# Attention and two mixtures of experts on one core: raw tiles, sums and differences of the 512-token round, its output units in pairs, and TensorE's order as the code emits it

## The chip, the core and the metric

The kernel runs on one core of a Trainium2 chip. The metric is the device time of one execution in microseconds. Five engines work side by side and in order, each through its own queue of instructions: PE (TensorE, matmuls), ACT (ScalarE), DVE (VectorE), POOL (GpSimd) and SP (SyncE, which here only issues DMAs). They wait for each other by semaphores. TensorE runs at 2.4 GHz when the throttle grants it its full clock, which is shown as 1.00.

## The reference, cut to what matters

Packed attention gives 2304 tokens of 512 numbers, a first layer with a squared relu follows, and then a mixture of eight experts, of which this change touches one part:

```
x = attention(q, k, v, p); x = (relu(x @ w_in) ** 2) @ w_out
logits = x @ w_gate;  P = exp(logits - logits.max())
for _ in range(8):
    P /= P.sum(1) + 1e-09;  P /= P.sum(0) + 1e-09;  P *= N / E
for e in range(E):                       # 8 experts
    h = relu(x @ w1[e])                  # 512 -> 1024
    out += P[:, e:e+1] * (h @ w2[e])     # 1024 -> 512
```

## The kernel before

Numbers are kept to fp32 accuracy by splitting each operand in two fp32r parts, a high part (a copy on ACT) and a low part (a subtraction on POOL or DVE). A product is then three matmuls: high by high, high by low, low by high.

The mixture of experts runs in three rounds of tokens: 512, 768 and 1024. Each round goes through 32 units n = 0 to 31, four to an expert. The change lies in the first round ("the 512-token round", p = 0), which on the timeline runs from about 418 to 776 us. It is also the round in which the weights w1 and w2 come in raw, are summed, split and put away (kept) for the other rounds, and in which the gate P is balanced.

A unit multiplies by Strassen's scheme in Winograd's form: seven block products instead of eight, from sums of weight blocks (S1 to S4, made by `w1_sums`) and differences of token blocks (T1 to T4, made in `operand`, line L466). Each product is six matmuls of 256 columns (L754) into the PSUM tiles X, Y or Z, in the order A11, A12, S1, S2, S4, S3, A22. Between them ACT copies partial results away (s: L815 after A11, L823 after S1, L826 after S2), DVE adds them back (L817 after A12, L830 after S4, L833 after S3), and `evac` makes the relu on ACT (L761) and its low part on DVE (L762), both in the tile hh. Those four hh tiles are the operands of the second layer's output units: `y_unit` makes six matmuls of 512 columns (L784) into one of four PSUM tiles of its own, and every fourth unit adds the sum, times the gate, to acc (L794 on DVE, L790 on ACT for the first expert). `ys` is the list of output units still to be done; `y()` takes one from it. It starts with five empty ones, so that a unit's outputs come one unit or so later.

After A12, S2, S3 and A22 the unit calls hook(n, 0) to hook(n, 3). The hooks issue what stands beside the products: the splits of weights for coming units (`split_w`: ACT L176, POOL L177), loads of raw weights (L111; from ACT's queue, apart from the first two), `sums_ahead` (four sums on DVE, L145 to L148, into one tile "wt"), the putting away of what is split (SP, L181), the operands for the next round (`keep_operand` in units 9 to 15: difference L466, copy L445, low part L446), and the gate. The gate takes the maximum of P in unit 1 (L696 on DVE, matmul L700, L701), spreads it in unit 2, and then balances in eight turns of two steps: `rows_step` on DVE (L714 to L719) and `cols_step` (matmul L724 by a matrix of ones, then L726 to L728 on DVE). Its matmuls take a PSUM tile of the same four ("c") that X, Y and Z turn through.

A scheduler orders each engine's instructions, by its own estimate of when they can run, except where the code says that an instruction comes after another: `pinned()` puts what it holds behind the last instruction so far of every engine. Products and output units are not held by it, so that the scheduler mixes them on PE. EARLY is 10: up to unit 9 sums and loads are placed by the hook itself.

## Time and profile before

| | before |
|---|---|
| median of 3 runs | 1858.34 us (1858.09 to 1859.39) |
| the profiled execution: time (its span, with nothing around it) | 1858.9 us |
| granted clock of TensorE, mean | 0.999 |
| busy share of the span: PE, weight loads, DVE, ACT, POOL | 99%, 89%, 69%, 45%, 56% |

The profile is of one execution, and its times count from the first instruction. A busy time of PE is made from records whose ends are modelled and that overlap with the next matmul, so the start of one group against the start of the next says more about its pace. An idle time is listed before the instruction that waited, with the instruction that released it.

### The profile page before, as it was taken

The numbers are of one execution on the slowest core, as the hardware profiler recorded it, in microseconds if no ns is written. First come the engines' busy times: TensorE is split into PE (matmuls) and PEld (weight loads), VectorE is DVE, ScalarE is ACT, GpSimd is POOL, SyncE is SP. The second block draws the span as 40 slices with busy tenths as digits, with TensorE's granted clock in tenths as the row PEclk, the third lists the DMA queues.
The fourth block names the chain that finished last, engine by engine and source line by source line (L and its number), as shares of the span: only waits on it lengthen the run. The fifth ranks groups of instructions, "written<-read, shape, count | busy, mean of one in ns | idle before, by whom it ended". The sixth has DMA issues, their size and how long they took to land.

```text
span 1858.9 us, 28526 instructions
## 1 busy us (share of the span) xinstructions
PE 1837.6 (99%) x10190; PEld 1663.2 (89%) x10190; DVE 1279.4 (69%) x2097; ACT 829.4 (45%) x1538; POOL 1047.0 (56%) x653
## 2 busy tenths in 40 slices
PE   8999999999999999999999999999999999999999
PEld 7899999998888898888888888888889999999998
DVE  4777777766766555588778877888775666666665
ACT  6667654644555555343333433333334323332323
POOL 3313322435688777278778777778764444444444
PEclk9999999999999999999999999999999999999999
DMA  7402211206789887767777787776788777788874
GB/s 277 159 27 77 69 46 47 103 2 229 252 317 325 299 271 255 243 219 257 234 249 233 233 267 233 238 238 228 248 307 268 276 258 266 258 245 265 267 251 148
DMA packets 166124, 403.55 MB, mean 217 GB/s; under 512 B 14192, under 2 KB 79712, under 8 KB 165984
## 3 DMA queue, kind: packets, MB, share of 16 engines
q1 hardware_dynamic: 131520, 346.15, 55.1%
q10 hardware_dynamic: 34464, 55.58, 9.8%
q8 instruction: 81, 1.33, 0.3%
q14 instruction: 59, 0.48, 0.1%
HBM read 273.96 MB, written 127.72 MB: 216 GB/s over the span
## 4 chain that ended last, share of the span: by engine, by line
PE 91%; DVE 3%; DMA 2%; issue 1%; ACT 1%; POOL 1%; SPq 0%; ACTq 0%; POOLq 0%; DVEq 0%
PE psc L754 35%; PE psx L1141 16%; PE psz L1141 12%; PE psy L430 11%; PE psy L784 7%; PE psh L411 6%; PE psh L364 1%; PE pp L270 1%; DMA raw<-win 1%; POOL w L177 1%; DMA raw<-w 1%; PE s L304 0%; PE s L238 0%; ACT w L176 0%; DMA kt<-kT 0%
## 5 line engine op out<-in xcount | busy, mean ns | idle before, releaser
L754 PE MATMUL psc<-xc,w 128*128 128x256 f32 (+2 forms) x4032 | 777.4, 335 | 2.3 <-ACT s L823 1.6
L754 PEld LDWEIGHTS psc<-xc,w 128*128 128x128 f32 x4032 | 666.3, 188 | 67.5 <-ACT s L823 1.8
L1117 POOL TENSOR_TENSOR hh<-hb,hh 128x1024 fp32r<-128x1024 f32 (+1 forms) x224 | 504.6, 2257 | 372.1 <-ACT hh L1116 314.4
L1116 ACT ACTIVATE hh<-hb 128x1024 fp32r<-128x1024 f32 (+1 forms) x224 | 213.8, 955 | 447.8 <-DVE hb L1114 197.8
L1141 PE MATMUL psx<-hh,wa 128*128 128x512 f32 (+1 forms) x1536 | 352.7, 362 | 0.0
L1141 PEld LDWEIGHTS psx<-hh,wa 128*128 128x128 f32 x1536 | 278.9, 188 | 30.2 <-ACT hh L1116 0.4
L1141 PE MATMUL psz<-hh,wa 128*128 128x512 f32 (+1 forms) x1152 | 261.9, 362 | 0.3 <-issue 0.3
L1141 PEld LDWEIGHTS psz<-hh,wa 128*128 128x128 f32 x1152 | 209.0, 188 | 23.2 <-issue 0.9
L430 PE MATMUL psy<-h,w 128*128 128x320 f32 (+2 forms) x1200 | 224.8, 331 | 0.2
L784 PE MATMUL psy<-w,hh 128*128 128x512 f32 x768 | 201.5, 395 | 3.9 <-ACT hh L761 3.3
L177 POOL TENSOR_TENSOR w<-raw,w 128x512 fp32r<-128x512 f32 (+1 forms) x128 | 157.9, 1255 | 76.9 <-ACT w L176 66.0
L1149 DVE TENSOR_TENSOR acc<-psx,acc 128x512 f32<-128x512 f32 (+1 forms) x248 | 152.1, 618 | 70.2 <-PE psx L1141 69.0
L430 PEld LDWEIGHTS psy<-h,w 128*128 128x128 f32 x1200 | 189.0, 188 | 12.2 <-ACT x L436 0.7
L1149 DVE TENSOR_TENSOR acc<-psz,acc 128x512 f32<-128x512 f32 (+1 forms) x184 | 112.6, 618 | 93.1 <-PE psz L1141 93.0
L1047 DVE SCALAR_TENSOR_TENSOR hb<-psc,gate 128x512 f32<-128x512 f32 (+1 forms) x256 | 157.3, 620 | 12.2 <-PE psc L754 7.3
L1021 POOL TENSOR_TENSOR wa<-rb,wa 128x512 fp32r<-128x512 f32 x80 | 132.6, 1666 | 49.9 <-ACT wa L1020 39.5
L784 PEld LDWEIGHTS psy<-w,hh 128*128 128x128 f32 x768 | 135.1, 189 | 27.8 <-ACT hh L761 4.6
L1114 DVE TENSOR_TENSOR hb<-hb 128x1024 f32<-128x1024 f32 (+1 forms) x96 | 133.5, 1390 | 28.9 <-POOL hh L1117 28.0
L411 PE MATMUL psh<-at,g 128*128 128x320 f32 (+2 forms) x768 | 123.4, 297 | 0.2 <-DVE r L417 0.2
L411 PEld LDWEIGHTS psh<-at,g 128*128 128x128 f32 x768 | 110.9, 189 | 4.3 <-DVE r L417 0.4
L177 POOL TENSOR_TENSOR w<-wt,w 128x512 fp32r<-128x512 f32 x64 | 83.7, 1316 | 47.8 <-ACT w L176 35.9
L129 POOL TENSOR_TENSOR ca<-ca,cc 128x512 int32<-128x512 int32 x28 | 36.7, 1311 | 102.6 <-ACT cc L128 94.1
(155 smaller groups left out, 1843.3 us busy)
## 6 DMA issues: line engine op xcount, KB each, us to landing
w<-kept_w SPq DMA_DIRECT2D x184, 512.0 KB, 4.8
kept_w<-wa SPq DMA_DIRECT2D x112, 512.0 KB, 4.6
wa<-kept_w SPq DMA_DIRECT2D x112, 512.0 KB, 4.8
kept_w<-w SPq DMA_DIRECT2D x96, 512.0 KB, 4.7
raw<-w ACTq DMA_DIRECT2D x58, 512.0 KB, 5.2
rb<-w ACTq DMA_DIRECT2D x64, 256.0 KB, 4.5
w<-kept_w SPq DMA_DIRECT2D x61, 256.0 KB, 4.3
raw<-win SPq DMA_DIRECT2D x16, 512.0 KB, 3.9
```

What stands on the lines that cost most here:

```text
L177: nc.gpsimd.tensor_tensor(w[:, 1, :n], t, w[:, 0, :n].bitcast(F32), op=ALU.subtract)
L411: nc.tensor.matmul(ps[:, u - begin:w - begin], gw[:, x, m * 128:(m + 1) * 128], at[:, y, g, u - b * S:w - b * S], start=(i == 0), stop=(i ...
L430: nc.tensor.matmul(ps[:, :n], w[:, x, d * 128:(d + 1) * 128], h[:, y, :], start=(i == 0), stop=(i == 11))
L754: last = nc.tensor.matmul(ps[:, :N], w[:, u, o + k * 128:o + (k + 1) * 128], x[v][:, k, :], start=(start and k + u + v == 0), stop=(k == 1 ...
L784: nc.tensor.matmul(ps, h[:, x, o:o + 128], w[:, y, :], start=(n % 4 + m + x + y == 0), stop=(n % 4 == 3 and m == 1 and x == 1), skip_group ...
L1021: nc.gpsimd.tensor_tensor(w[:, 1], src, w[:, 0].bitcast(F32), op=ALU.subtract)
L1047: nc.vector.scalar_tensor_tensor(HB[q][m, t][:, nn, :], src, 0.0, GATE[p, g // 4][:, t * N:(t + 1) * N], op0=ALU.max, op1=ALU.mult)
L1114: nc.vector.tensor_tensor(src, src, hb[MINUS[k]], op=ALU.subtract)
L1116: nc.scalar.activation(hi, src, AF.Copy)
L1117: nc.gpsimd.tensor_tensor(lo, src, hi.bitcast(F32), op=ALU.subtract)
L1141: nc.tensor.matmul(ps, A2[q, k][:, u, nn, d * 128:(d + 1) * 128], OPS[7 * q + k][v][:, nn, :], start=(first and nn + u + v == 0), stop=(nn ...
L1149: nc.vector.tensor_tensor(a, ps, a, op=ALU.add)
```

## The change

It has five parts, all in the 512-token round.

1. Raw tiles: six places for raw weights instead of four. The two new ones are halves of a tile `raws` in the pool `hq`. Four loads, no longer two, are issued ahead of the round, on SP's queue.
2. Sums: kept by the number n of the unit they belong to; those of odd units 3 to 9 go into a second tile (the place "x6"). Those of units 2 and 3 are made in hooks 0 and 1 of unit 0, and those of n + 2 in hook 1 of unit n (before: of n + 1).
3. Differences: for the operands of the next round the subtraction (now `difference`) is made in hook 2 of units 9 to 15, the copy and the low part in hook 3 as before.
4. Output units: two after S2 and two after S3. Before there was one each after A12, S2, S3 and A22.
5. TensorE's order: `last_pe()` puts every product of units 1 to 31 of this round, and every output unit, behind the last PE instruction that the code has issued so far.

```diff
-        where = stage if more is None or (k - more[0]) % 4 >= 2 else more[1]
-        t = where.tile([128, 512], I64, tag="raw", name="raw64", bufs=2) if kind == "f64" else \
-            where.tile([128, 1024], F32, tag="raw", name="raw", bufs=2)
-        (nc.sync if more is None or k < more[0] + 2 else nc.scalar).dma_start(t, src)
+        place = 4 if more is None else (k - more[0]) % 6
+        if place in (2, 3):
+            t = more[2][:, place - 2, :]
+        else:
+            where = stage if place > 3 else more[1]
+            t = where.tile([128, 512], I64, tag="raw", name="raw64", bufs=2) if kind == "f64" else \
+                where.tile([128, 1024], F32, tag="raw", name="raw", bufs=2)
+        (nc.sync if more is None or k < more[0] + 4 else nc.scalar).dma_start(t, src)
...
-        t = wpools[2].tile([128, 1024], F32, tag="wt", name="wt", bufs=1)
+        t = xcb.tile([128, 1024], F32, tag="x6", name="wt", bufs=1) if n % 2 and 2 < n < EARLY else \
+            wpools[2].tile([128, 1024], F32, tag="wt", name="wt", bufs=1)
...
-    def sums_ahead(ahead=0):
-        w1_sums(raw[splits[state["split"] + ahead][1]])
+    def sums_ahead(n):
+        w1_sums(next(l for key, l, _ in splits if key == ("w1", n, 0)), n)
...
+    def difference(p, name):
+        if name in SUM:
             u, v = (x_block(p, *PLACE[x]) for x in SUM[name])
             nc.vector.tensor_tensor(x_block(p, *PLACE[name]), u, v, op=ALU.subtract)
+
+    def operand(p, name, t, engine, ready=False):
+        if (p, name) != (0, "T4") and not ready:
+            difference(p, name)
         split_x(p, name, engine, t)
...
     def product(ps, n, p, a, b, start):
+        if p == 0 and n > 0:
+            with last_pe():
+                return one_product(ps, n, p, a, b, start)
+        return one_product(ps, n, p, a, b, start)
...
+    def last_pe():
+        return tc.issue_after(next(i for i in reversed(nc.cur_bb.bb.instructions) if i.engine == mybir.EngineType.PE))
...
         def y():
             if ys:
-                ys.pop(0)()
+                with last_pe():
+                    ys.pop(0)()
...
         evac((n, p, 0, 0), Y, p)
-        y()
         after.get(0, lambda x: None)(at)
...
         after.get(1, lambda x: None)(at)
         y()
+        y()
         product(Z, n, p, "S4", "B22", False)
...
         after.get(2, lambda x: None)(at)
         y()
+        y()
         at = product(X, n, p, "A22", "T4", False)
         evac((n, p, 1, 0), X, p)
         after.get(3, lambda x: None)(at)
-        y()
...
-    state["more"] = state["load"], rx
-    load_w()
-    load_w()
+    state["more"] = state["load"], rx, hq.tile([128, 2, 1024], F32, tag="hb", name="raws", bufs=1)
+    for _ in range(4):
+        load_w()
...
     for k in range(7):
+        extra[9 + k, 2] = lambda k=k: difference(1, ORDER[k])
         extra[9 + k, 3] = lambda k=k: keep_operand(ORDER[k], k)
...
-            if i > 1:
+            if i < 2:
+                with pinned():
+                    sums_ahead(2 + i)
+            else:
                 with pinned():
                     if i == 2:
                         split_w(2)
-                        sums_ahead()
...
-                if n == 1 and i == 0:
-                    sums_ahead(2)
                 if 1 < n < EARLY and i == 1:
-                    sums_ahead()
+                    sums_ahead(n + 2)
                 if n == EARLY and i == 0:
-                    sums_ahead(4)
+                    sums_ahead(n + 2)
```

The added lines shift the line numbers: a product's matmul is L769 in the changed kernel (L754 before), an output unit's L799 (L784), relu and low part L776 and L777 (L761, L762), the adds L836, L849, L852 (L817, L830, L833), the sums L150 to L153 (L145 to L148), the difference L471 (L466), the gate's matmuls L709 and L733 (L700, L724), `rows_step` L723 to L728 (L714 to L719).

The instructions of PE in unit 4 of the round, where the name of a product's operand tells the product (xc_4181 is A11 and A12, xc_4364 S1 and S2, xc_4182 S4 and S3, xc_4365 A22). Before:

```order
L754 MATMUL psc<-xc_4181,w 128x256 x6
L784 MATMUL psy<-w,hh 128x512 x6
L754 MATMUL psc<-xc_4181,w 128x256 x6
L784 MATMUL psy<-w,hh 128x512 x8
L754 MATMUL psc<-xc_4364,w 128x256 x6
L724 MATMUL psy<-cs,ones 128x8
L754 MATMUL psc<-xc_4364,w 128x256 x6
L784 MATMUL psy<-w,hh 128x512 x6
L754 MATMUL psc<-xc_4182,w 128x256 x12
```

And now, PE in the same unit:

```order
L769 MATMUL psc<-xc_4181,w 128x256 x12
L733 MATMUL psy<-cs,ones 128x8
L769 MATMUL psc<-xc_4364,w 128x256 x12
L799 MATMUL psy<-w,hh 128x512 x12
L769 MATMUL psc<-xc_4182,w 128x256 x12
L799 MATMUL psy<-w,hh 128x512 x12
```

The gate's matmul moved from between S1 and S2 to between A12 and S1, and the output matmuls from between A11, A12 and S1 to two places. Unit 6 reads the same.

DVE from the end of unit 3 into unit 4 (hh is the low part after a relu, psc<-psc,s an add, rs and cs the gate's row step, cr its column step). Before:

```order
L762 SCALAR_TENSOR_TENSOR hh<-psc,hh 128x256
L714 TENSOR_REDUCE rs<-P 128x18
L715 TENSOR_SCALAR rs<-rs 128x18
L716 RECIPROCAL rs<-rs 128x18
L717 TENSOR_TENSOR P<-P,rs 128x144
L719 TENSOR_REDUCE cs<-P 128x8
L817 TENSOR_TENSOR psc<-psc,s 128x256
L762 SCALAR_TENSOR_TENSOR hh<-psc,hh 128x256
L726 TENSOR_SCALAR cr<-psy 128x8
```

And now, DVE at the same place:

```order
L777 SCALAR_TENSOR_TENSOR hh<-psc,hh 128x256
L723 TENSOR_REDUCE rs<-P 128x18
L724 TENSOR_SCALAR rs<-rs 128x18
L836 TENSOR_TENSOR psc<-psc,s 128x256
L725 RECIPROCAL rs<-rs 128x18
L726 TENSOR_TENSOR P<-P,rs 128x144
L777 SCALAR_TENSOR_TENSOR hh<-psc,hh 128x256
L728 TENSOR_REDUCE cs<-P 128x8
L735 TENSOR_SCALAR cr<-psy 128x8
```

The reduction to cs, which the gate's matmul reads, moved behind unit 4's first add and the low part after it.

DVE in unit 0, from its first add on (wt is the tile of sums). Before, from the copy ahead of it:

```order
L509 COPY lgT<-psl 32x256
L145 TENSOR_TENSOR wt<-raw 128x256
L147 TENSOR_TENSOR wt<-raw 128x256
L817 TENSOR_TENSOR psc<-psc,s 128x256
L146 TENSOR_TENSOR wt<-wt,raw 128x256
L148 TENSOR_TENSOR wt<-raw,wt 128x256
L762 SCALAR_TENSOR_TENSOR hh<-psc,hh 128x256
L830 TENSOR_TENSOR psc<-psc,s 128x256
L833 TENSOR_TENSOR psc<-psc,s 128x256
```

And now, DVE from the same copy:

```order
L518 COPY lgT<-psl 32x256
L836 TENSOR_TENSOR psc<-psc,s 128x256
L777 SCALAR_TENSOR_TENSOR hh<-psc,hh 128x256
L150 TENSOR_TENSOR wt<-raw 128x256
L152 TENSOR_TENSOR wt<-raw 128x256
L151 TENSOR_TENSOR wt<-wt,raw 128x256
L849 TENSOR_TENSOR psc<-psc,s 128x256
L153 TENSOR_TENSOR wt<-raw,wt 128x256
L852 TENSOR_TENSOR psc<-psc,s 128x256
```

The sums moved from around the first add to behind the first low part, ahead of the second and third add.

## Rows read from the trace of the kernel before

**Rows 1.** The page's head: span, and busy time of each engine.

```profile
span 1858.9 us, 28526 instructions
...
PE 1837.6 (99%) x10190; PEld 1663.2 (89%) x10190; DVE 1279.4 (69%) x2097; ACT 829.4 (45%) x1538; POOL 1047.0 (56%) x653
```

**Rows 2.** Windows: length, busy time by engine, clock, DMA share, GB/s.

```profile
430.00:440.00 10.00, 8.07 (x44) 6.65 (x42) 6.69 (x8) 5.13 (x13) 10.00 (x9) 1.00 0.87 311
...
600.00:610.00 10.00, 8.38 (x52) 7.16 (x51) 8.57 (x15) 4.16 (x10) 7.99 (x6) 1.00 1.03 404
...
420.00:780.00 360.00, 354.14 (x2188) 316.25 (x2189) 213.15 (x460) 188.76 (x439) 241.71 (x191) 1.00 0.80 274
```

**Rows 3.** Waits of PE, 410 to 790: total, times, longest.

```profile
PE psy L784 <- ACT hh L761: 3.3, 6, 2.1
PE psc L754 <- ACT s L823: 1.6, 1, 1.6
PE psy L784 <- DVE acc L794: 0.4, 1, 0.4
PE psc L754 <- ACT s L815: 0.3, 1, 0.3
```

**Rows 4.** Timeline, 430 to 446: start, length, engine and group.

```profile
432.58 3.12 PE L784 MATMUL psy<-w,hh 128*128 128x512 f32 x13
...
433.53 5.02 POOL L177 TENSOR_TENSOR w<-raw,w 128x256 fp32r<-128x256 f32 x4
...
434.48 1.51 DVE L147 TENSOR_TENSOR wt<-raw 128x256 f32<-128x256 f32 x1
...
435.54 1.60 PE L754 MATMUL psc<-xc,w 128*128 128x256 f32 x12
...
436.97 1.09 PE L784 MATMUL psy<-w,hh 128*128 128x512 f32 x4
...
439.77 0.36 ACT L761 ACTIVATE hh<-psc 128x256 fp32r<-128x256 f32 x1
...
440.19 1.20 PE L784 MATMUL psy<-w,hh 128*128 128x512 f32 x4 [2.12 <-ACT hh L761]
...
441.23 0.87 PE L754 MATMUL psc<-xc,w 128*128 128x256 f32 x6
441.31 0.29 DVE L696 TENSOR_REDUCE gmx<-P 128x1 f32<-128x144 f32 x1
```

**Rows 5.** The chain of waits, 590 to 607.

```profile
592.03 6.64 DMA raw<-w
...
601.57 1.64 DVE x L466
...
604.68 1.69 PE psc L754 x12
```

**Rows 6.** Timeline of DVE, 454 to 480.

```profile
455.06 1.33 DVE L717 TENSOR_TENSOR P<-P,rs 128x144 f32<-128x144 f32 x1
...
459.28 0.43 DVE L817 TENSOR_TENSOR psc<-psc,s 128x256 f32<-128x256 f32 x1 [0.86 <-PE psc L754]
460.16 0.42 DVE L762 SCALAR_TENSOR_TENSOR hh<-psc,hh 128x256 fp32r<-128x256 f32 x1 [0.45 <-ACT hh L761]
...
461.68 0.44 DVE L719 TENSOR_REDUCE cs<-P 128x8 f32<-128x144 f32 x1
462.13 0.43 DVE L145 TENSOR_TENSOR wt<-raw 128x256 f32<-128x256 f32 x1
```

**Rows 7.** Timeline of ACT, 454 to 480.

```profile
459.74 0.39 ACT L761 ACTIVATE hh<-psc 128x256 fp32r<-128x256 f32 x1 [0.87 <-DVE psc L817]
...
463.61 0.63 ACT L176 ACTIVATE w<-wt 128x512 fp32r<-128x512 f32 x1
```

**Rows 8.** Timeline of PE, 454 to 480: the gate's matmul.

```profile
470.83 0.29 PE L724 MATMUL psy<-cs,ones 128*128 128x8 f32 x2
```

**Rows 9.** Groups of DVE, 418 to 776: busy, mean; idle before, releasers.

```profile
L830 DVE TENSOR_TENSOR psc<-psc,s 128x256 f32<-128x256 f32 x32 | 13.8, 431 | 61.4 <-PE psc L754 59.6 <-ACT w L176 1.5
```

More of the change, by code (lines that the diff above doesn't have):

```diff
@@ L138, with w1_sums @@
     sums = {}
-    def w1_sums(r):
-        a11, a12, a21, a22 = (r[:, j * 256:(j + 1) * 256] for j in range(4))
-        t = wpools[2].tile([128, 1024], F32, tag="wt", name="wt", bufs=1)
+    def w1_sums(l, n):
+        a11, a12, a21, a22 = (raw[l][:, j * 256:(j + 1) * 256] for j in range(4))
+        t = xcb.tile([128, 1024], F32, tag="x6", name="wt", bufs=1) if n % 2 and 2 < n < EARLY else \
+            wpools[2].tile([128, 1024], F32, tag="wt", name="wt", bufs=1)
         s1, s2, s3, s4 = (t[:, j * 256:(j + 1) * 256] for j in range(4))
@@ L148, in w1_sums, with w1_blocks @@
         nc.vector.tensor_tensor(s4, a12, s2, op=ALU.subtract)
-        sums["t"] = t
-    def w1_blocks(r, n, i):
+        sums[n] = t
+    def w1_blocks(l, n, i):
         if i == 0 and not 2 <= n < EARLY + 3:
-            w1_sums(r)
-        return (r[:, 0:512], sums["t"][:, 0:512], sums["t"][:, 512:1024], r[:, 768:1024])[i]
-    def sums_ahead(ahead=0):
-        w1_sums(raw[splits[state["split"] + ahead][1]])
+            w1_sums(l, n)
+        return (raw[l][:, 0:512], sums[n][:, 0:512], sums[n][:, 512:1024], raw[l][:, 768:1024])[i]
+    def sums_ahead(n):
+        w1_sums(next(l for key, l, _ in splits if key == ("w1", n, 0)), n)
     def split_w(n=1):
@@ L173, in split_w @@
             else:
-                t = w1_blocks(raw[l], key[1], i)
+                t = w1_blocks(l, key[1], i)
             n = t.shape[1]
@@ L461 @@
     SUM = {"T1": ("B12", "B11"), "T2": ("B22", "T1"), "T3": ("T2", "B11"), "T4": ("B21", "T2")}
-    def operand(p, name, t, engine):
-        if name in SUM and (p, name) != (0, "T4"):
+    def difference(p, name):
+        if name in SUM:
             u, v = (x_block(p, *PLACE[x]) for x in SUM[name])
             nc.vector.tensor_tensor(x_block(p, *PLACE[name]), u, v, op=ALU.subtract)
+    def operand(p, name, t, engine, ready=False):
+        if (p, name) != (0, "T4") and not ready:
+            difference(p, name)
         split_x(p, name, engine, t)
@@ L746, in product, with one_product @@
     def product(ps, n, p, a, b, start):
+        if p == 0 and n > 0:
+            with last_pe():
+                return one_product(ps, n, p, a, b, start)
+        return one_product(ps, n, p, a, b, start)
+    def one_product(ps, n, p, a, b, start):
         i, o = WHERE[a]
@@ L870, in keep_operand @@
         t = xc_tile(1, xcb, f"x{4 + i % 3}")
-        operand(1, name, t, nc.vector if i % 2 else nc.gpsimd)
+        operand(1, name, t, nc.vector if i % 2 else nc.gpsimd, True)
         KEPTX[name] = kept.tile([128, 2, 2, GROUPS[1][1]], F32R, name=f"kept_x_{name}")
```

## The prediction

> **What bounds the kernel now.** I read the page's head first: TensorE is busy for 1837.6 of 1858.9 us [rows 1]. Then the windows over the 512-token round, the only place where anything moves: PE is busy for 354.14 of its 360 us at a granted clock of 1.00 [rows 2]. So 5.86 us of idle is all there is, 1.93 of it in 430 to 440 and 1.62 in 600 to 610. The waits name it: output matmuls L784 for the ACT copy of hh (six waits, 3.3 us, the longest 2.1), one product for s (L823), 1.6, and two small ones [rows 3]; that is nine waits and 5.6 us.
>
> A wait costs more than its idle time, since matmuls overlap. Start to start, thirteen L784 take 2.96 us (432.58 to 435.54), 0.228 each, and twelve L754 1.43 (435.54 to 436.97), 0.119 each. Across the long wait the four L784 from 436.97 and the four from 440.19 took 4.26 us up to 441.23, where eight at 0.228 need 1.82: 2.44 lost for 2.12 idle [rows 4]. So I add 0.3 to each wait: 2.4 us for the first, and for the other eight 3.74 + 8 x 0.3 = 6.1. **What can be had is 8.5 us, 0.46% of the time.** Matmuls are neither added nor taken away (24 x 0.228 + 42 x 0.119 = 10.5 us in a unit of the round, before and after).
>
> Where the two long waits come from. At 433 DVE's four sums, one of them 1.51 us long, run beside four POOL splits of 5.02 us together; the relu at 439.77 stands behind them and L784 starts at 440.19 [rows 4]. Before 604 a raw load takes 6.64 us, the difference L466 then 1.64, and s (L823) is late behind the operand copy L445 [rows 5].
>
> **What the change removes.** Both chains are cut: two more raw tiles make a load start two turns earlier, the sums come two units ahead, and the differences leave the hook where copy and split follow them. The six hh waits arise where an L784 was put right behind the add and the relu that it needs. In the new order the pairs stand behind S2 and S3 and belong to units already finished, so their hh is old. I take all nine waits as gone: **-8.5** (bounds -5, if late operands stay late, and -9.5, with the hitches under 0.1 us that the wait view does not list). The extra loads and the second sums tile add no instruction; DVE, ACT and POOL do what they did, under TensorE's cover, at 69%, 45% and 56% busy [rows 1]. If a set of sums loses that cover, it costs 1.7 us alone (four at 0.43, [rows 6]) or, with all four at the 1.51 of [rows 4], 6.0.
>
> **What it adds.** Before, the scheduler filled a late product's place with output matmuls. Now products and output units stand as written, and between them stand the gate's small matmuls. Each of those waits for DVE, and everything behind it on TensorE waits too.
>
> *Units 4 and 6, L733* (L724 before). The order rows show it between A12 and S1. The reduction L728 that feeds it stands on DVE behind the add L836 of that same A12 and the split L777 behind it. Rows of the same chain: add from 459.28, split done at 460.16 + 0.42, so 1.30 us; the reduction (L719 before) 0.44 [rows 6]; the relu between them is at 459.74, and one w split, 0.63, may stand ahead of it on ACT, 0.2 more than the add covers [rows 7]. 1.30 + 0.44 + 0.2 = 1.94. PE could have started the next matmul 0.16 before its last one's recorded end (six take 0.87 by record, 0.71 by start [rows 4]), and restarts lose 0.1: **2.2 each, 4.4 for both**. Before, the same reduction stood ahead of the add, and L724 of this unit ran at 470.83 without a wait [rows 8]. Bounds: 1.9 without the split; 3.2 if the product L726 (L717 before) takes 1.33 us, as at 455.06 [rows 6].
>
> *Unit 1, L709* (L700 before): pinned behind S3 with no output unit ahead of it. It needs add, relu and split of that S3 (1.30) and the maximum L705 (0.29, [rows 4]): 1.59 + 0.16 + 0.1, **1.9** (1.6 to 3.0).
>
> *Units 0 and 1.* The first sums now stand on DVE ahead of the third add of unit 0, and its A22 writes the bank which that add reads. There are no output units to fill with. Four sums at 0.43 and two adds at 0.43 follow the first split, 2.6 us, and S4 and S3 cover 1.43 of it: 1.2, and 0.3 for a restart: **1.5**. In unit 1 the copy s1 stands behind four w splits on ACT, 2.5 us by [rows 7], with about 1.4 of product ahead: **1.0**. Bounds for the two together: 0.5 and 4.
>
> *L733 behind A22 of units 2, 4 and 6* needs the five row instructions, 460.58 to 462.12 in [rows 6], 1.54 us, behind add, relu and split: 2.84. Twelve output matmuls and A22 cover 2.74 + 0.71 - 0.16 = 3.29. Hidden, with 0.4 to spare; one L726 of 1.33 gives 0.6 of wait. I take **0.5** for the three (0 to 4.5).
>
> *The later units.* From unit 12 on I find no exposed wait: with twelve output matmuls (2.74 us) behind S2 and again behind S3, each of the three adds and the four splits has over a microsecond. In units 10 to 16 the operand copy can hold s1 by 0.2 at times; nothing is taken for it.
>
> **Sum.** -8.5 + 4.4 + 1.9 + 1.5 + 1.0 + 0.5 = +0.8 on the profiled execution's 1858.9, 1859.7. That one lies 0.56 above the median of the three runs, 1858.34, so a median of 1859.1: I say **1859.0**. Within 0.2% (3.7 us) is about what a measurement cannot tell from no change.
>
> **Rivals.**
>
> *The gate matmuls' waits are not paid (faster).* If DVE and ACT, freed of late sums, ran ahead so that L733 and L709 found their operands, only some 2.5 us of the new terms would be left: -8.5 + 2.5 = -6, 1852.3. For it: DVE idles 59.6 us in the round in front of the add L830, waiting for PE [rows 9], so it has time. Against it: time does not help an instruction that stands behind an add of the product just done. It decides from new waits below 4.8 us in sum. Chance 0.30.
>
> *Sums beside POOL come back as a wait (slower).* Before, the scheduler let adds in between the sums; now units 2 to 9 put four sums, with nothing between, ahead of the second and third add. From A12 to A22, products and pairs take 4 x 0.71 + 2 x 2.74 = 8.3 us. On DVE lie first split 1.3, column steps 0.9, four sums and two adds 0.9: 4.8 with sums at 0.43, but 9.1 with sums at 1.51 [rows 4]. Then A22 waits 0.8, and the L733 behind it 1.5 or more. Four of eight sets so hit are 4 x 1.5 = 6 on top of the sum: 1865. It decides from about three sets. In [rows 4] all four sums were slow beside POOL; at 462.13 the first took 0.43 with POOL idle [rows 6]. The Trainium skill, "SBUF — State Buffer", section "Who interferes with whom", says that a VectorE instruction with two SBUF inputs and a GpSimd instruction that reads SBUF exclude each other for a whole instruction. By it each sum next to a split would cost the rest of one split more, which the 1.51 beside 5.02 / 4 = 1.26 us splits agrees with; were every set beside splits, the sum would be some 8 x 1.5 = 12 us worse, by an estimate. POOL is busy for 242 of the 360 us [rows 2], so some sets must meet it. Chance 0.23.
>
> *The order was not what made PE wait (no change).* If the load at 592 is late in the new order as well and the sums still meet POOL in unit 1, about 4 of the 8.5 us stay, but then fewer of the new waits show, since they fall in the same places: -4.5 + 5 = +0.5, 1858.8. Nothing in the time tells it from my forecast; the trace would. I count it with mine: 0.47 for both.
>
> **How the numbers follow.** The forecast's own bounds: removed -9.5 to -5, added 6 to 13; half of each spread on either side gives 1856 to 1862.5. The range must reach towards both rivals: 1853.5 leaves out about 0.1 below (the first rival with nothing else paid), 1863.0 about 0.1 above. Faster by over 0.2% means under 1854.6: 0.28 (the first rival, and a little less, since part of it ends above). Slower means over 1862.1: 0.22. The same: 0.50.
>
> **What would show it.** Right: no L799 waits for hh anywhere in the round; nothing at 600 to 610; PE waits at L733 twice for about 2 us with DVE L728 as releaser (around 20 us apart), once at L709 (releaser L705), once at an L769 in the first ten microseconds. Wrong in the direction of faster: L733 and L709 start with no idle time, PE over 99.5% busy from 440 to 780. Wrong in the direction of slower: sums L150 to L153 over 1 us each in most sets, adds L849 and L852 late, L769 of A22 waiting for them, or waits in units 10 to 31, where I took none.

## The result, and the profile after

The change takes 1878.13 us, the median of four runs (1876.05 to 1879.71), against 1858.87 for four runs of the kernel before on the same chip: ratio 1.0102, interval 1.009 to 1.0114. It is 19.3 us slower, and the forecast was 1859.0 with a range up to 1863.0. The page's head of the changed kernel, beside [rows 1]:

```profile
span 1877.7 us, 28545 instructions
...
PE 1845.7 (98%) x10190; PEld 1671.0 (89%) x10190; DVE 1313.5 (70%) x2097; ACT 833.4 (44%) x1538; POOL 1045.1 (56%) x653
```

The span grew by 18.8 us, with the same number of matmuls. PE is busy for 8.1 us longer over the same work, DVE for 34.1 us longer, and ACT and POOL hardly differ. So three things are to be found: PE's new idle time, why its matmuls take longer, and what fills DVE.

PE's waits in the round, from 410 to 800, beside [rows 3]:

```profile
PE psc L769 <- ACT s L841: 4.7, 3, 2.1
PE psc L769 <- ACT s L834: 4.2, 3, 1.8
PE psy L733 <- DVE cs L728: 3.7, 3, 1.8
PE psc L769 <- DVE psc L852: 3.1, 2, 2.7
PE psy L709 <- DVE gmx L705: 1.8, 1, 1.8
PE psc L769 <- DVE hh L777: 0.4, 1, 0.4
```

The nine waits of before are gone: no output matmul (L799) waits for anything. In their place stand thirteen others, 17.9 us against 5.6. Five of these (three at L733, one at L709, and the 2.73 of L852) are the ones that the prediction costed; the s copies L834 and L841 are not.

Windows of the changed kernel, with the columns of [rows 2]:

```profile
420.00:430.00 10.00, 7.27 (x57) 6.90 (x56) 6.65 (x15) 4.06 (x12) 2.69 (x2) 0.97 0.40 146
430.00:440.00 10.00, 8.24 (x46) 7.30 (x45) 3.35 (x9) 6.00 (x15) 9.60 (x9) 0.84 0.88 301
440.00:450.00 10.00, 10.00 (x56) 8.83 (x55) 4.75 (x8) 4.54 (x12) 5.42 (x6) 0.84 0.75 278
470.00:480.00 10.00, 10.00 (x51) 8.72 (x51) 4.89 (x15) 5.20 (x11) 5.08 (x4) 0.83 0.66 234
490.00:500.00 10.00, 8.21 (x55) 7.40 (x54) 6.12 (x20) 5.08 (x12) 6.50 (x7) 1.00 0.68 241
...
620.00:630.00 10.00, 7.90 (x44) 6.97 (x43) 7.37 (x11) 3.35 (x10) 6.02 (x5) 0.87 0.60 209
```

In [rows 2] the granted clock of the whole round was 1.00. Here it is below that in five stretches of ten microseconds shown, and at 0.96 from 630 to 640: ten times the missing parts, 0.3 + 1.6 + 1.6 + 1.7 + 1.3 + 0.4, makes 6.9 us. Of ten microseconds at 0.84, a little over three were at 1.2 GHz instead of 2.4. The windows at 440 and 470 have no idle time, yet they lose 1.6 and 1.7 us. What stood ahead of them, in PE's timeline of the changed kernel:

```profile
438.30 0.38 PE L709 MATMUL psy<-ident,gmx 128*1 128x128 f32 x2 [1.75 <-DVE gmx L705]
438.61 4.58 PE L799 MATMUL psy<-w,hh 128*128 128x512 f32 x12
...
469.26 0.39 PE L733 MATMUL psy<-cs,ones 128*128 128x8 f32 x2 [1.79 <-DVE cs L728]
469.51 2.15 PE L769 MATMUL psc<-xc,w 128*128 128x256 f32 x12
471.46 4.04 PE L799 MATMUL psy<-w,hh 128*128 128x512 f32 x12
...
494.74 0.39 PE L733 MATMUL psy<-cs,ones 128*128 128x8 f32 x2 [1.79 <-DVE cs L728]
494.98 1.68 PE L769 MATMUL psc<-xc,w 128*128 128x256 f32 x12
```

Behind the stops of 1.75 and 1.79 us twelve output matmuls, part of them at 1.2 GHz, take 4.58 and 4.04 us, where twelve at the full clock take 2.91 (below, at 621.94). Behind the equal stop at 494.74 the clock stays at 1.00. So a stop can cost nearly twice its length, or only its length.

What fills DVE are the four sums of a weight. First the groups of the third and the first of them before, from 418 to 790, then the same two sums in the changed kernel (number, then busy time and mean ns). There 20 of the 30 stand in these groups; the other ten read the new tile `raws`, and take 1294 and 877 ns:

```profile
L147 DVE TENSOR_TENSOR wt<-raw 128x256 f32<-128x256 f32 x30 | 16.9, 563 | 0.0
...
L145 DVE TENSOR_TENSOR wt<-raw 128x256 f32<-128x256 f32 x30 | 15.4, 514 | 21.0 <-POOL w L177 18.4 <-DMA raw<-w 2.6
```

```profile
L152 DVE TENSOR_TENSOR wt<-raw 128x256 f32<-128x256 f32 x20 | 22.6, 1128 | 0.0
L150 DVE TENSOR_TENSOR wt<-raw 128x256 f32<-128x256 f32 x20 | 17.5, 874 | 7.9 <-POOL w L182 6.2 <-DMA kept_w<-w 1.6
```

All 120 sums took 71.7 us before and take 107.4 now, at 0.42 each when nothing disturbs them. The mean of before was already 0.60: it met POOL too, but less (18 of the 120 took over 1 us then, 48 now). Here is the longest of the three waits for s (L841), in the timeline of all engines at 620:

```profile
619.89 2.73 POOL L182 TENSOR_TENSOR w<-raw,w 128x512 fp32r<-128x512 f32 x2
619.96 1.51 DVE L150 TENSOR_TENSOR wt<-raw 128x256 f32<-128x256 f32 x1
...
621.39 1.51 DVE L152 TENSOR_TENSOR wt<-raw 128x256 f32<-128x256 f32 x1
...
621.94 2.91 PE L799 MATMUL psy<-w,hh 128*128 128x512 f32 x12
622.58 2.17 POOL L182 TENSOR_TENSOR w<-raws,w 128x256 fp32r<-128x256 f32 x2
...
623.49 1.54 DVE L151 TENSOR_TENSOR wt<-wt,raw 128x256 f32<-128x256 f32 x1
...
625.62 0.42 DVE L836 TENSOR_TENSOR psc<-psc,s 128x256 f32<-128x256 f32 x1
626.07 0.38 ACT L776 ACTIVATE hh<-psc 128x256 fp32r<-128x256 f32 x1 [4.74 <-DVE psc L836]
...
626.51 0.38 ACT L841 ACTIVATE s<-psc 128x256 f32<-128x256 f32 x1
...
626.95 1.26 PE L769 MATMUL psc<-xc,w 128*128 128x256 f32 x6 [2.10 <-ACT s L841]
```

Read it upwards. The product waits for the copy s at 626.51. That copy needs nothing that is late: it stands behind the relu at 626.07 in ACT's queue, and ACT has idled for 4.74 us in front of that relu, which waits for the add L836. The add stands on DVE behind four sums, three of which take 1.5 us, each beside one of POOL's subtractions (L182). Twelve output matmuls cover 2.91 us, and no more stand there. The same chain stands at 692 (1.04 us of wait) and at 736 (1.61, where a difference of 1.98 us is in it as well).

The waits for the copy s of L834 come by other ways along ACT's queue. At 519 (1.84 us) four scalings of acc stand ahead of it:

```profile
515.95 2.56 ACT L808 ACTIVATE acc<-acc,P 128x512 f32<-128x512 f32 x4 [1.36 <-DVE P L737]
```

At 586 (1.18 us), and alike at 610 (1.19), a raw load does, which ACT's queue issues:

```profile
582.16 0.33 ACTq L115 DMA_DIRECT2D raw<-w  x1
582.54 0.38 ACT L776 ACTIVATE hh<-psc 128x256 fp32r<-128x256 f32 x1 [1.83 <-POOL w L182]
...
585.95 0.39 ACT L834 ACTIVATE s<-psc 128x256 f32<-128x256 f32 x1
...
586.39 0.98 PE L769 MATMUL psc<-xc,w 128*128 128x256 f32 x6 [1.18 <-ACT s L834]
```

The load is released by a subtraction that POOL ends at 582.12, and ACT idles until then. Seven more instructions of ACT stand between that relu and the copy. The subtraction itself was late because its split stood behind a relu that had waited 3.26 us for an add on DVE, behind three sums of 1.40 to 1.55 us.

### The profile page after: what moved, and what is told of

It reads as the page before. It is cut to its first block, busy times and chain, and to the rows that moved or that the text cites. A ratio compares the mean times of both kernels' runs of the same rounds, so it can differ in the third digit from the quotient of the medians.

```text
span 1877.7 us, 28545 instructions
## 1 busy us (share of the span) xinstructions
PE 1845.7 (98%) x10190; PEld 1671.0 (89%) x10190; DVE 1313.5 (70%) x2097; ACT 833.4 (44%) x1538; POOL 1045.1 (56%) x653
## 4 chain that ended last, share of the span: by engine, by line
PE 64%; DVE 2%; DMA 0%; POOL 0%; issue 0%; ACT 0%; ACTq 0%; POOLq 0%; DVEq 0%
PE psc L769 32%; PE psx L1161 16%; PE psz L1161 12%; PE psy L799 4%; PE pso L1184 0%; DVE wt L152 0%; DMA raw<-w 0%; POOL w L182 0%; DVE wt L150 0%; DVE wt L151 0%; DVE rb L1038 0%; DVE hb L1067 0%; DMA kept_w<-w 0%; DVE x L471 0%; DVE rb L1037 0%
## 5 line engine op out<-in xcount | busy, mean ns | idle before, releaser
L769 PE MATMUL psc<-xc,w 128*128 128x256 f32 (+2 forms) x4032 | 772.0, 337 | 12.8 <-ACT s L841 4.7
L769 PEld LDWEIGHTS psc<-xc,w 128*128 128x128 f32 x4032 | 660.5, 190 | 75.2 <-ACT s L841 6.0
L799 PE MATMUL psy<-w,hh 128*128 128x512 f32 x768 | 190.3, 397 | 0.0
L799 PEld LDWEIGHTS psy<-w,hh 128*128 128x128 f32 x768 | 142.6, 192 | 27.5 <-issue 0.2
L182 POOL TENSOR_TENSOR w<-raw,w 128x512 fp32r<-128x512 f32 x88 | 107.0, 1232 | 95.7 <-ACT w L181 55.9
L182 POOL TENSOR_TENSOR w<-wt,w 128x512 fp32r<-128x512 f32 x64 | 83.5, 1317 | 32.7 <-ACT w L181 21.9
L777 DVE SCALAR_TENSOR_TENSOR hh<-psc,hh 128x256 fp32r<-128x256 f32 x128 | 53.7, 421 | 68.3 <-ACT hh L776 67.3
```

The source lines that it names most:

```text
L182: nc.gpsimd.tensor_tensor(w[:, 1, :n], t, w[:, 0, :n].bitcast(F32), op=ALU.subtract)
L769: last = nc.tensor.matmul(ps[:, :N], w[:, u, o + k * 128:o + (k + 1) * 128], x[v][:, k, :], start=(start and k + u + v == 0), stop=(k == 1 ...
L799: nc.tensor.matmul(ps, h[:, x, o:o + 128], w[:, y, :], start=(n % 4 + m + x + y == 0), stop=(n % 4 == 3 and m == 1 and x == 1), skip_group ...
```

## The experiments

My theory after the two traces: the order now written is what costs, because TensorE can't step round a late operand, and what makes operands late there are the gate's matmuls where they now stand, sums lengthened beside POOL, and stops behind which the clock falls. The rivals: the moved loads, sums and differences cost by themselves; the fixed order costs whatever DVE does; or POOL's length costs, not its meeting with DVE. Ratios are to the kernel before on the same chip; waits are PE's, from 410 to 800.

**Parts 1 to 3 alone** (units unpaired too):

```diff
-        if p == 0 and n > 0:
-            with last_pe():
-                return one_product(ps, n, p, a, b, start)
...
-                with last_pe():
-                    ys.pop(0)()
+                ys.pop(0)()
```

> The raw tiles, the sums two units ahead and the moved differences alone; output units at the four old places and TensorE's order left to the scheduler. Theory P (the fixed order costs: each late operand now stops TensorE, and the clock falls behind the longest stops): the time is that of before or a little less, 1853 to 1860 us, fewer than six waits on TensorE in the round and the granted clock 1.00 throughout. Theory L (the moved sums and differences make VectorE late, the order only shows it): 1865 us or more, with waits for s or hh after 600 us.

1859.61 us, ratio 1.0001 (0.9992 to 1.001), clock 1.00 throughout. There are ten waits, all short, where I expected fewer than six. The long waits for s are gone, but waits for hh come back in the scheduler's order:

```profile
PE psy L796 <- ACT hh L773: 2.2, 6, 1.0
PE psy L796 <- DVE hh L774: 2.1, 2, 1.1
```

So the moved loads, sums and differences cost nothing, and gain nothing either, in the old order.

**Parts 4 and 5 alone**, on the kernel before: `last_pe()` and the pairs added there.

> Pairs of output units and TensorE's order as emitted, with the old raw tiles, sums and differences. Theory P: as slow as the change or slower, 1873 to 1890 us, with over 15 us of idle on TensorE in the round and stretches at half clock. Theory L: within 3 us of before, 1856 to 1862.

1886.53 us, ratio 1.0144 (1.0129 to 1.016). One stop of 4.9 us for the gate's maximum is followed by a stretch at clock 0.66 from 440 to 450. In the written order the earlier sums and loads thus save some 8 us: they do what they do, but less than that order takes.

**The order without the pairs**: the changed kernel, output units one each at the four old places, all pinned.

```diff
         evac((n, p, 0, 0), Y, p)
+        y()
...
         y()
-        y()
```

> The change with output units one at a time at the four old places, in a fixed order. If the pairs' 2.7 us between dependent products are needed: 1884 us or more, with waits behind S2 and S3 in most units. If the fixed order alone sets the cost: 1874 to 1882 us. Less than 1872 if an output unit behind A12 covers the waits of L733.

1878.94 us, ratio 1.0103 (1.0088 to 1.0118), the same as the change. The pairs are not the cause; pinning is, for this run and parts 1 to 3 differ in nothing else that the code says. The scheduler's order of DVE moves with the pinning, though: from unit 12 on this run and the change have eight sums in every second unit and hardly any in the next, where parts 1 to 3 have three to five in most.

**The gate's matmuls step back**: products and output units are put behind the last product or output unit issued, and no longer behind a gate's matmul, and the gate's step moves to another hook in every second unit.

```diff
-        return tc.issue_after(next(i for i in reversed(nc.cur_bb.bb.instructions) if i.engine == mybir.EngineType.PE))
+        return tc.issue_after(state.get("mm") or next(i for i in reversed(nc.cur_bb.bb.instructions) if i.engine == mybir.EngineType.PE))
...
-            if n > 2 and i != 1 or (n, i) == (2, 3):
+            if n > 2 and i != n % 2 or (n, i) == (2, 3):
```

> The change, but products and output units are held only behind each other, no longer behind the gate's small matmuls, and the column steps of units 4 and 6 are issued after S2 instead of after A12. If the waits at L709 and L733 are lost time of their own and pull the clock down behind them: they go (5.5 us of idle, 1.2 of restarts), and two of the four stretches at half clock with them (3.1 us): 1867 to 1870 us. If TensorE would only meet the next late operand instead: 1875 us or more.

1874.82 us, ratio 1.0084 (1.0069 to 1.0099). I expected 1867 to 1870, a miss. The wait at L709 is gone and L733 waits for 2.2 us instead of 3.7 (a new wait of 0.8 stands at L715), but the waits for s and L852 are where they were, and the clock now falls behind others of them (0.83 from 510 to 520 and from 620 to 630). So the early gate is the smaller part.

**POOL's subtraction replaced by a memset** (the low part of the weights is left out in this round):

```diff
-            nc.gpsimd.tensor_tensor(w[:, 1, :n], t, w[:, 0, :n].bitcast(F32), op=ALU.subtract)
+            if state.get("more"):
+                nc.gpsimd.memset(w[:, 1, :n].bitcast(F32), 0.0)
+            else:
+                nc.gpsimd.tensor_tensor(w[:, 1, :n], t, w[:, 0, :n].bitcast(F32), op=ALU.subtract)
```

> The change, but in this round GpSimd fills the low parts of the weights with zeros instead of subtracting: its instructions no longer read SBUF, and the low parts are left out of the result. Theory C (sums beside GpSimd's subtractions take about 1.5 us each, and the add behind them is late): all sums at 0.42 us, the three waits for s5 behind output units at 625, 691 and 735 us gone (4.7 us of idle) with the stretch at half clock at 627: 1868 us or less. Rival (ScalarE's own queue order makes s5 late): those three waits stay, 1874 us or more.

1859.85 us, ratio 1.0007 (0.9997 to 1.0016). One of its groups of sums, and PE's waits:

```profile
L152 DVE TENSOR_TENSOR wt<-raw 128x256 f32<-128x256 f32 x20 | 8.3, 417 | 0.0
```

```profile
PE psy L736 <- DVE cs L731: 3.6, 2, 1.8
PE psy L712 <- DVE gmx L708: 1.8, 1, 1.8
PE psc L772 <- DVE psc L855: 0.9, 1, 0.9
PE psc L772 <- ACT s L837: 0.7, 1, 0.7
```

The third sum takes 0.42 (1.13 in the same group above), and four of the 120 take over 1 us instead of 48. No wait is left from 500 on to the end of the units, and the gate's remain. This takes away 18 us of the 19. Three other things move with it: POOL's work is shorter (100 us of the 360 instead of 240), POOL no longer reads the raw tiles, and the scheduler orders DVE otherwise. As to the last, four sums still stand between the third add of the unit before and the first adds of units 17, 23 and 27, where the change waited for L841; at 0.42 they make nothing late. POOL's length is what the runs with the sums on POOL take apart.

**The same memset in the kernel before.**

> The kernel before, with GpSimd filling the low parts of the weights with zeros in this round (left out of the result). If sums beside GpSimd's subtractions were also what made TensorE wait before, its two long waits (2.1 and 1.6 us) go and the time is 1853 to 1856 us. If the scheduler's order left little of it to lose: within 2 us of before.

1853.66 us, ratio 0.9967 (0.9954 to 0.998), with 1.6 us of waits. So the subtractions, with the lengthened sums, cost the old order 6 us as well. Between these two kernels, without them, the change still costs 1859.85 - 1853.66 = 6.2 us.

**Gate stepped back, and the memset**; the scaling of the output accumulator (the four instructions at 516 above) is also issued behind ACT's last instruction, an edit that no run has by itself.

> The change with all that the runs so far blame taken out: GpSimd writes zeros for the low parts of the weights (left out of the result), products are not held behind the gate's matmuls, the column steps of units 4 and 6 come behind S2, ScalarE's scaling of acc behind its last copy. Theory C (the fixed order is harmless by itself; it exposes what the slowed sums and the gate make late): at most 4 us of lag in the round, clock 1.00, 1852 to 1856 us, as fast as the kernel before with zeros (1853.7) or faster. Rival (a fixed order loses by itself, since nothing fills a wait): 1858 us or more.

1852.54 us, ratio 0.9965 (0.9952 to 0.9978), with 2.0 us of waits at a clock of 1.00. With operands in time the written order costs nothing that shows: it is level with the kernel before without subtractions (0.9967). "The fixed order costs whatever DVE does" falls.

**Sums in halves**: two sums in one hook, two in a later one, pinned in the later units too, so that an add can come between.

```diff
-        nc.vector.tensor_tensor(s1, a21, a22, op=ALU.add)
...
+        if half == 0:
+            nc.vector.tensor_tensor(s1, a21, a22, op=ALU.add)
+            nc.vector.tensor_tensor(s2, s1, a11, op=ALU.subtract)
+        else:
+            nc.vector.tensor_tensor(s3, a11, a21, op=ALU.subtract)
+            nc.vector.tensor_tensor(s4, a12, s2, op=ALU.subtract)
```

> The change, with each unit's four sums in two halves: two behind the low part after S3 or after A12, two in the next such place, so that no add stands behind more than two of them. GpSimd's subtractions stay. Theory C (four sums beside GpSimd's subtractions take up to 6 us and make the next add late): the three waits for s5 at 625, 691 and 735 us go, the one of unit 0 is halved, and the stretches at half clock behind these go too: some 10 us less than the change, 1866 to 1870. Rival (the total of the slowed sums counts, not where they stand): 1874 us or more.

1876.52 us, ratio 1.009 (1.0075 to 1.0105), a miss: 1866 to 1870 was expected. The three waits for the copy s of L841 are gone and the one in unit 0 falls from 2.73 to 1.61, but another takes their place:

```profile
PE psc L775 <- ACT s L840: 8.6, 9, 2.0
```

That is the copy s which was L834 in the change: a weight split whose sum is not yet made now stands ahead of it on ACT. The late sum was moved from one in-order queue to another.

**Halves, gate stepped back, and the scaling** of the run above, without the memset.

> As the run before, and products held only behind each other and not behind the gate's matmuls, the column steps of units 4 and 6 behind S2, and ScalarE's scaling of acc behind its last copy. If waits, and the clock that falls behind the longest, are all that the change adds: 1857 to 1862 us, two or three waits of about 1 us left (L733, L715) and the granted clock 1.00. If the next late operand takes each place: 1866 us or more. Below 1855 only if hardly any wait is left.

1865.99 us, ratio 1.0035 (1.0021 to 1.005), 4 us above the range that I hoped for. Two thirds of the loss are gone with the full work done. Most of what is left is eight waits for that s, 7.2 us. In ACT's timeline the split stands ahead of it and has waited 2.17 us for its sum:

```profile
729.57 0.63 ACT L187 ACTIVATE w<-wt 128x512 fp32r<-128x512 f32 x1 [2.17 <-DVE wt L152]
730.11 0.37 ACT L844 ACTIVATE s<-psc 128x256 f32<-128x256 f32 x1
```

**The gate's stops filled**: eleven spare matmuls into an unused part of the gate's bank ahead of L709 and of L733 in units 4 and 6.

```diff
+            for _ in range(11):
+                nc.tensor.matmul(b[:, 256:512], W["w1", n, 0][:, 0, 0:128], XC[0, "B11"][0][:, 0, :], start=True, stop=True,
+                                 skip_group_check=True)
```

> The change, with eleven matmuls that nobody reads (1.3 us) put into each of the three waits for the gate, ahead of L709 and of the L733 of units 4 and 6; nothing else moves. If TensorE's clock falls because it stood still there: the waits keep their end, two stretches at half clock (at 440 and 471 us, 3.1 us together) go, and the time is 1874 to 1876 us. If the clock falls for another reason, or falls elsewhere instead: within 1.5 us of the change, 1877 to 1880.

1877.73 us, ratio 1.01 (1.0083 to 1.0117): its time can't be told from the change's. In its trace the low stretches at 440 and 470 are gone, but that from 430 to 440 (0.84, behind the wait of 2.73) and that from 620 to 630 (0.83) remain. The traced executions differ by 2.9 us (spans of 1874.8 and 1877.7), the medians by 0.4. Inconclusive for the time; what it shows is that with the stops at those two places filled the clock stayed at 1.00 behind them.

**Sums on POOL**, in this round, with the subtractions kept: no DVE sum is left to meet POOL, and POOL has more to do.

```diff
-        nc.vector.tensor_tensor(s1, a21, a22, op=ALU.add)
+        (nc.gpsimd if state.get("more") else nc.vector).tensor_tensor(s1, a21, a22, op=ALU.add)
```

(and the other three alike). First on the changed kernel:

> The change with one edit: GpSimd makes the four sums of this round, not VectorE, so that the two engines no longer read SBUF against each other there; GpSimd gets 120 more instructions of about 0.75 us and its subtractions stay. Theory C (two engines slowing each other makes the adds late): the waits for s5 at 625, 691 and 735 us and most of unit 0's go, the waits for the gate (5.4 us) stay: 1862 to 1868 us. Rival (zeros helped because GpSimd was done sooner with each part): GpSimd has more to do than ever, waits for w appear and the time is 1878 us or more.

1874.94 us, ratio 1.0086 (1.0071 to 1.0101), a miss: 1862 to 1868 was expected. The waits of the later units, from 520 to 800, do fall, from 7.8 us in the change (4.7 of them for L841) to these:

```profile
PE psc L769 <- ACT s L834: 2.2, 3, 0.9
PE psc L769 <- POOL w L182: 0.7, 1, 0.7
PE psc L769 <- DVE psc L852: 0.6, 1, 0.6
```

The three waits for L841, behind the late add, are gone although POOL is now busy for 314.40 of 360 us, where it was 240.32. So POOL's length did not make that add late; and as the memset has the four sums in front of it at 0.42 without a wait, it was their length, beside POOL. The copies L834 still cost 2.2 us, which this run leaves open. The time hardly falls because the early gate's matmuls now wait 9.1 us instead of 3.7.

**Sums on POOL, gate stepped back, and the scaling:**

> The same with products not held behind the gate's matmuls, the column steps of units 4 and 6 behind S2 and the scaling of acc behind ScalarE's last copy. Theory C: little is left, 1853 to 1858 us, clock 1.00. Rival: 1868 us or more.

1863.58 us, ratio 1.0027 (1.0016 to 1.0038), with 9.3 us of waits, a miss: 1853 to 1858 was expected. By the ratios these edits together save some 14 us (0.0075 of 1859), where the gate and the sums alone saved some 3 each (0.0018 and 0.0016): with only one of them, the other's stops and the clock behind them remain. What the scaling adds to this is not taken apart.

**Sums on POOL in the kernel before:**

> The kernel before with the sums of this round on GpSimd. Theory C: like the kernel before with zeros, 1853 to 1856 us. Rival (GpSimd becomes late): 1860 us or more, with waits for w.

1869.27 us, ratio 1.0054 (1.0039 to 1.0069): worse, where 1853 to 1856 was expected, with one stop of 6.6 us at 702 and the clock at 0.72 and 0.77 behind it. PE waits there for the third add, which stands on DVE behind the low part of an operand:

```profile
700.07 7.75 DVE L446 TENSOR_TENSOR xc<-x,xc 128x1024 fp32r<-128x1024 f32 x1 [4.39 <-ACT xc L445]
```

Such a low part takes 1.22 us on average in the kernel before; here it runs beside POOL's sums and subtractions, with POOL at 87%. Moving the sums is no gain as such: the meeting comes back at another instruction of DVE.

**Two attempts at a better order**, built on the halves with the gate stepped back: weight splits spread otherwise, raw loads a hook later and differences two hooks earlier; in the second the early gate's step is also issued ahead of the sums, with its memset made early.

```diff
-        split_w(((0, 2, 3, 1) if n == 1 else (2, 1, 2, 1) if n < EARLY else (2, 2, 1, 1))[i])
+        with pinned():
+            split_w(((0, 2, 3, 1) if n == 1 else (2, 1, 1, 2) if n < EARLY else (2, 2, 1, 0) if n == EARLY else (1, 2, 3, 0))[i])
...
-        extra[9 + k, 2] = lambda k=k: difference(1, ORDER[k])
+        extra[9 + k, 0] = lambda k=k: difference(1, ORDER[k])
```

> The change with the order of ScalarE's and VectorE's work written out as well: the sums in halves, the weight splits behind the copies that TensorE waits for, raw loads issued one hook after their place came free, the differences in hook 0, the gate as in the run before; GpSimd subtracts. If standing order around the slowed sums is all that is needed: waits under 6 us in sum, clock 1.00, 1853 to 1859 us. If the slowed sums always make something late: 1864 us or more.

1875.72 us, ratio 1.009 (1.0075 to 1.0105). From 510 on only 2.8 us of waits are left, but the early gate is worse:

```profile
PE psy L739 <- DVE cs L734: 8.2, 3, 3.5
PE psy L721 <- DVE grow L716: 5.0, 1, 5.0
```

> As the run that wrote out ScalarE's and VectorE's order (1875.72 us), with the gate's work ahead of the sums and splits in the hooks of the first nine units, and the row that the gate's maximum is written into cleared ahead of the round. That run lost 17 us in front of three gate matmuls and at half clock behind them. If these were due to the sums ahead of the gate alone: 1857 to 1861 us, as fast as the kernel before with the subtractions in place. If the slowed sums then make another operand late: 1865 us or more.

1865.2 us, ratio 1.0035 (1.0021 to 1.0049), at a clock of 1.00 throughout. The stop of 5.0 us is gone, 10.3 us of waits remain, and it is not the 1857 to 1861 that I hoped for. No version with the whole work beat the kernel before.

**A ledger over the runs.** For each profiled execution: PE's idle time from 410 to 800 and the number of waits, the clock's loss (ten times what the windows of ten microseconds lack to 1.00), and the span less 1858.9. The sum is (idle - 5.6) + 0.3 for each wait more than nine + the clock's loss.

| Kernel | idle, waits | clock | sum | span, difference |
|---|---|---|---|---|
| the change | 17.9, 13 | 6.9 | +20.4 | +18.8 |
| parts 1 to 3 | 5.0, 10 | 0 | -0.3 | -1.0 |
| parts 4, 5 | 22.8, 13 | 10.2 | +28.6 | +27.5 |
| order without pairs | 17.9, 13 | 5.1 | +18.6 | +16.5 |
| gate back | 15.5, 12 | 5.1 | +15.9 | +14.1 |
| memset | 7.3, 6 | 3.4 | +4.2 | +2.0 |
| memset, before | 1.6, 6 | 0 | -4.9 | -7.2 |
| gate back, memset | 2.0, 3 | 0 | -5.4 | -8.1 |
| halves | 16.1, 14 | 5.1 | +17.1 | +16.9 |
| halves, gate back | 10.6, 12 | 1.8 | +7.7 | +5.3 |
| filled | 14.0, 13 | 3.4 | +13.0 | +15.9 |
| sums on POOL | 17.9, 14 | 3.4 | +17.2 | +14.9 |
| the same, gate back | 9.3, 10 | 1.7 | +5.7 | +3.3 |
| the same, before | 12.0, 12 | 5.1 | +12.4 | +8.3 |
| first attempt | 17.2, 8 | 6.8 | +18.1 | +14.9 |
| second attempt | 10.3, 11 | 0 | +5.3 | +5.4 |

The sum follows the span to within 4.1 us everywhere. Idle time and clock account for the differences here. Two rows need care: the traced execution of the memset took 1862.68 us, 2.8 above its median, and in the row filled the 3.9 us that spare matmuls fill are lost all the same, though they no longer count as idle.

## Why the prediction was wrong

**What bounds the kernel, and -8.5.** Right. No L799 waits for hh, and all nine waits are gone.

**The early terms, +9.3.** Right in sum. They came as five waits of 8.2 us (1.75 at L709, 1.79 twice and 0.17 at L733, 2.73 at the first A22); with 0.3 for each wait, 9.7. The gate's terms were right one by one. That the whole sum came out so near is partly luck, for two terms were off and nearly cancel: the first A22 has 3.0 instead of 1.5, since two of the four sums ahead of it took 1.50 and 1.15, and the copy s1 of unit 1 has no wait where 1.0 was taken.

**"From unit 12 on I find no exposed wait."** This is the step that failed. From unit 12 on there are seven waits of 7.8 us, with 0.3 each 9.9. An eighth, the 1.84 us at 519, falls into unit 8, for which the sum has no term either. Together they are 17.9 - 8.2 = 9.7 us, with 0.3 each 12.1. I gave adds and splits over a microsecond of room with the sums at 0.43, and had read the new order of DVE for units 0, 3 and 4 only, not for units 12 to 28 with their eight sums in every second one. The timeline at 620 shows four sums from 619.96 to the add at 625.62, and the output matmuls cover 2.91 of it. Also, I followed each add to the product that reads its bank, and not along ACT's queue, where the copy s of another product stands behind the relu that waits for that add. For the three waits at L841, 4.7 us, the runs show that sums lengthened beside POOL make them. The other five go with the memset too, and lengthened sums stand in the chain at 586, but there POOL's hold on the raw tiles and, at 519, the scalings are in it as well, and no run parts them.

**The clock, no term.** The sum had no place for the 6.9 us that TensorE lost behind the new stops. [Rows 4] had a stop of 2.12 us, and [rows 2] show 1.00 over the round, so I took a stop to cost its length.

-8.5 + 9.7 + 12.1 + 6.9 = 20.2, of 18.8 in the span.

**The rivals.** "Sums beside POOL come back as a wait" named the mechanism. It was placed at the third add of units 2 to 9 and priced at 6 us; it came out mainly at the copies s of units 8 to 27 and in unit 0, for about twice that, and the clock on top. In the Trainium skill, "SBUF — State Buffer", section "Who interferes with whom", a VectorE instruction with two SBUF inputs contends with a GpSimd instruction that reads SBUF, over a port pair that is an exclusive lock. The trace agrees: at 620 three sums take 1.5 us, each beside one subtraction, and the same sums take 0.42 with the memset. The rule was in the prediction and given a chance of 0.23; what it lacked was the reason why more sums meet subtractions now (120 sums in 107.4 us instead of 71.7). That eight of them stand in one unit is a small part of it at most: the halves have four in each of these units, and their 120 sums still take 98.8 us. Before, the first of a set idled 18.4 us in all for POOL, in the group L145 above, and now 6.2 in one group and 2.0 in the other. That fits sums that start while POOL is at work instead of behind it, but no run moved that alone. That the gate's waits would not be paid is wrong: they were, in full.

**What would show it.** L733 twice (25 us apart, not 20), L709 once and L769 some ten microseconds into the round came as written. "Nothing at 600 to 610" did not, and sums over 1 us with waits in units 10 to 31, named as the sign of the slower case, are what the trace shows.

**What each part costs.** By medians against the kernel before: without the meeting the change costs 6.2 us (memset against memset), and that is mainly the early gate with its clock: 5.4 of the 7.3 us of waits left with the memset are the gate's, and with the gate stepped back and the scaling moved all of it is gone (1852.54 against 1853.66). The other 13 come only where the written order and POOL's subtractions stand together. Of these the L841 waits are shown to be lengthened sums; how the rest divides between lengthened sums and POOL's hold on the raw tiles stays open. Still open too: whether some written order with the whole work reaches the kernel before, and why the sums now fall together with the subtractions more often.

## What to carry to other kernels

When an order is pinned that a scheduler had filled, price every small instruction at its worst duration in the trace, not at its usual one, because the engine can no longer step round a late operand. Follow each late result along all the in-order queues: a copy that needs nothing late waits behind a relu that does. Read the order of the engines that were not pinned as well, over the whole stretch, because the scheduler moves their work too. And give each new stop as long as these a price for the clock too, because it can cost nearly as much again behind it.

## What the runs showed of the hardware

TensorE's clock fell to its lower level behind the stops of 2.73, 1.75, 1.79 and 2.10 us of the changed kernel (at 428, 438, 469 and 627), for about three microseconds each, but not behind those of 1.79 at 494, 1.84 at 519 and 1.61 at 736, nor behind the 2.12 of [rows 4]. Length alone does not decide it. Twelve output matmuls that ran in part at the lower level took 4.04 to 4.58 us instead of 2.91.

A sum of 128x256 on DVE takes 0.42 us alone and 1.50 beside POOL's subtractions. The add of the same shape whose operands are psc, which lies in PSUM, and s took 0.42 in between (426.52, inside the POOL group from 425.02 to 427.71):

```profile
425.02 2.69 POOL L182 TENSOR_TENSOR w<-raw,w 128x512 fp32r<-128x512 f32 x2 [8.52 <-PE psc L769]
425.10 1.50 DVE L151 TENSOR_TENSOR wt<-wt,raw 128x256 f32<-128x256 f32 x1
426.52 0.42 DVE L849 TENSOR_TENSOR psc<-psc,s 128x256 f32<-128x256 f32 x1
426.85 1.15 DVE L153 TENSOR_TENSOR wt<-raw,wt 128x256 f32<-128x256 f32 x1
```

The Trainium skill, "SBUF — State Buffer", section "Who interferes with whom", has a VectorE instruction with at most one SBUF input, outside the 2-port modes, as free of GpSimd, and one row here agrees.
